# Weight splits by pairs of tiles, and attention steps by two chunks, in a fused attention and feed-forward kernel

## The chip, the cores and the metric

The kernel runs on one core of a Trainium2 chip. Its engines work in parallel, each through its own queue in order: TensorE (PE in the rows; PEld is its weight load), VectorE (DVE), ScalarE (ACT), GpSimd (POOL) and SyncE (SP), which here only issues transfers. The metric is the device time of one execution in microseconds.

## The reference

The program is a Performer attention layer followed by two feed-forward layers, on 4 batches of 8 heads with 576 tokens of width 64:

```python
def phi(x):                                   # 128 random features
    h = einsum('bhsd,md->bhsm', x, omega) - sum(x * x) / 2
    return exp(h - max(h)) / sqrt(m)
q_p, k_p = phi(q * scale), phi(k * scale)
kv = einsum('bhsm,bhsd->bhmd', k_p, v);  z = sum(k_p, axis=2)
x = (q_p @ kv) / (q_p @ z + 1e-6)             # then 2304 tokens x 512
x = ((x @ w_a) * (x @ w_b)) @ w_out           # 512 -> 1536 -> 512
h = maximum(x @ w_in, 0);  out = (h * h) @ w_out2    # 512 -> 2048 -> 512
```

The weights arrive as float64, all else as float32, and the result is float32.

## The kernel before

**Precision.** A product runs over high and low parts in a fast float32 format: three products (high-high, high-low, low-high, `TERMS`) make one. Every weight tile (128 rows, 512 values) is therefore split on the chip into such a pair by `split` (line 120): a load brings the raw 64-bit words as pairs of 32-bit integers, then three ScalarE and five VectorE instructions of 512 columns each make the high part `t[:, 0]` and the low part `t[:, 1]`, with three cut tiles `u`, `a` and `p` on the way (two buffers each). The raw tiles have two buffers too (`rawp`, line 79), each for one tile.

**Stages.** The first feed-forward layer works on 9 blocks of 256 tokens, in passes (`PASSES`, line 543): blocks 0 to 2 with the first six of twelve f tiles, the same blocks with the last six, blocks 3 to 6 one by one, and blocks 7 and 8 together. In a pass each f has three units: products with `w_a`, products with `w_b` (both line 561, tiles `ab`), and the products with `w_out` of two f earlier (line 585, tile `y`). The second layer (`b_units`, lines 716 and 704) follows over all tokens.

**Attention beside it.** Attention is cut into lanes: `k_steps` makes the features of k for a pair of heads (four chunks of 128 tokens) and the sums `ps_kv`; `q_steps` makes the features of q, chunk by chunk: `proj`, then `feat` (two transposes, a copy `qT`), `num` (numerators `ps_n` and `quotient`), and `turn` (transposes into `x_all`, the input of the first layer; one `turn` serves the chunks that lie in one block, a "group"). The 64 tokens left of a sequence are the tail steps `kt_steps` and `qt_steps`. Some features go in full float32 (`WIDE`, line 33: `phi_wide`, a 128x256 product, a minimum over its columns, one exponential per head), the others by high and low parts (`proj`, line 293).

**Order.** Before the first pass, `start_lanes` runs the lanes that block 0 needs, and at every 12th step (`SD`, line 828) `get_first` loads and splits a weight tile. In the passes, `SIDES` (line 751) names the lanes that are spread over the units of a pass by their counted steps, `W_AT` how many weights are loaded in each, and in the last pass `get_w2` (line 795) loads one tile of the second layer's weights per unit. A scheduling layer sets the final order of each engine's queue from this code and from the buffers of each pool; a tile's next use waits until its last use has ended.

Of the kernel before, what the change touches and what calls it, by code (L numbers as in the profile page):

```python
# [10 lines left out]
I32 = mybir.dt.int32  # L11
# [33 lines left out]
def kernel(  # L45
# [59 lines left out]
    def load_cols(w, f):  # L105
        t = rawp.tile([128, 512, 2], I32, tag="raw", name="raw")
        nc.sync.dma_start(
            out=t.rearrange("p (k f) w -> p k (f w)", k=KC),
            in_=w[:, f * 256:(f + 1) * 256].rearrange("(k p) f -> p k f", p=128),
        )  # L110
        return t

    def load_rows(w, f):
        t = rawp.tile([128, 512, 2], I32, tag="raw", name="raw")
        nc.sync.dma_start(
            out=t.rearrange("p f w -> p (f w)"), in_=w[f * 128:(f + 1) * 128, :]
        )
        return t

    def split(raw, pool, tag):  # L120


        up = raw[:, :, 1]
        t = pool.tile([128, 2, 512], F32R, tag=tag, name=tag)
        u = cutp.tile([128, 512], F32, tag="u", name="u")
        a = cutp.tile([128, 512], F32, tag="a", name="a")
        p = cutp.tile([128, 512], F32, tag="p", name="p")
        nc.scalar.activation(out=a, in_=f32(up), func=ACTF.Copy, scale=WORD_SCALE)  # L128
        nc.vector.tensor_scalar(
# [7 lines left out]
        nc.scalar.copy(out=t[:, 0, :], in_=p)  # L137
        nc.scalar.activation(
            out=i32(u), in_=raw.bitcast(U16)[:, :, 1],
            func=ACTF.Copy, scale=2.0 ** 7,  # L140
        )
# [72 lines left out]
    def tail_turn(nm, b, g):  # L214

        ps = at_bank([128, 128], "ps_tt")
        nc.tensor.transpose(ps, tails[nm, b][:, g].rearrange("t h d -> t (h d)"), ident)
        st = ap2.tile([128, 128], F32, tag=f"T{nm}", name="T", bufs=1)
        nc.scalar.copy(out=st, in_=ps)
        return st  # L220

    def phi_wide(s, dst):

        nm = ap2.tile([128, 2], F32, tag="nm", name="nm", bufs=4)
        ps = at_bank([128, 2, M], "ps_p")
# [11 lines left out]
    class Side:  # L237
# [44 lines left out]
        def proj(self, i, dst):  # L282
# [15 lines left out]
            nc.scalar.copy(out=c, in_=ps[:, :, 1, :])  # L298
# [622 lines left out]
```

## Time and profile before

| what | value |
|---|---|
| time, median of 3 runs (lowest to highest) | 1080.52 us (1079.51 to 1081.36) |
| profiled execution: own time, span | 1076.06 us, 1074.3 us |
| TensorE busy | 1047.3 us, 97% of the span |
| VectorE busy | 554.1 us, 1546 instructions |
| ScalarE busy | 487.4 us, 1179 instructions |
| mean granted clock of TensorE | 0.993 |

The span runs from the first to the last instruction; the execution's own time also has what lies around it. A busy TensorE is not TensorE at its peak, since the ends of pipelined products are modelled. A granted clock of 1.00 is 2.4 GHz; where a stretch has less, the lower level of 1.2 GHz was granted in part of it. In the rows by stage the engines stand in the order TensorE, its weight loads, VectorE, ScalarE, GpSimd. In the chain of waits each piece is what the next one waited for, up to the end. A group of instructions has its count, its busy time and the mean of one.

### The profile page before, as it was taken

How to read it: one execution, taken by the hardware profiler on the slowest of the kernel's cores; microseconds unless marked ns; L12 is line 12 of the kernel's file. 1: busy time of each engine (PE TensorE's matmuls, PEld its weight loads, DVE VectorE, ACT ScalarE, POOL GpSimd, SP SyncE). 2: the span in 40 equal slices, each digit the busy share in tenths (PEclk: the TensorE clock that was granted, in tenths of full speed). 3: DMA queues.
4: the chain of work that ended last, by engine and by line, in shares of the span. 5: the costliest groups of instructions: out<-in, count | busy, mean ns of one | idle time of the engine just before them, and what ended most of it. 6: DMA issues, size and time to landing. Idle time of an engine off the chain costs nothing.

```text
span 1074.3 us, 17147 instructions
## 1 busy us (share of the span) xinstructions
PE 1047.3 (97%) x6505; PEld 928.2 (86%) x6505; DVE 554.1 (52%) x1546; ACT 487.4 (45%) x1179; POOL 29.2 (3%) x54
## 2 busy tenths in 40 slices
PE   5998999999999999999999999999999999999998
PEld 4797989999999999999998888788788788778887
DVE  5887888766655433444458878522322322222222
ACT  6886768654455533433346656422322322322232
POOL 3100101000000000000000000000000000000000
PEclk9998999999999999999999999999999999999999
DMA  7855875862543333333438665300200200100010
GB/s 190 237 139 181 237 239 166 269 186 89 157 129 101 92 123 124 118 109 103 124 108 268 221 188 160 96 0 1 79 1 1 69 1 1 49 1 0 1 41 20
DMA packets 105555, 118.64 MB, mean 110 GB/s; under 512 B 55808, under 2 KB 84480, under 8 KB 105472
## 3 DMA queue, kind: packets, MB, share of 16 engines
q1 hardware_dynamic: 103936, 115.96, 35.5%
q0 software_dynamic: 1536, 1.58, 0.6%
q8 instruction: 52, 0.85, 0.3%
q14 instruction: 31, 0.25, 0.1%
HBM read 100.20 MB, written 17.30 MB: 109 GB/s over the span
## 4 chain that ended last, share of the span: by engine, by line
PE 90%; DMA 3%; ACT 3%; DVE 2%; issue 1%; SPq 0%; ACTq 0%
PE ab L561 22%; PE o L704 18%; PE ph L716 17%; PE y L585 13%; PE abw L561 6%; PE ps_p L293 3%; PE ps_n L426 3%; PE ps_kv L365 3%; PE ps_p L226 2%; PE ps_qt L418 2%; DMA out_dram<-o_s 1%; PE ps_t L271 1%; DMA raw<-in_moe_w_b_dram 1%; PE ps_x L436 1%; DMA raw<-in_moe_w_a_dram 1%
## 5 line engine op out<-in xcount | busy, mean ns | idle before, releaser
L561 PE MATMUL ab<-x_all,w 128*128 128x256 f32 x2016 | 298.0, 292 | 0.4 <-DVE x_all L499 0.3
L561 PEld LDWEIGHTS ab<-x_all,w 128*128 128x128 f32 x2016 | 263.8, 191 | 2.1 <-DVE x_all L499 0.5
L716 PE MATMUL ph<-yx,w 128*128 128x512 f32 (+1 forms) x840 | 185.5, 371 | 0.0
L585 PE MATMUL y<-gs,wo 128*128 128x256 f32 (+1 forms) x1152 | 181.4, 302 | 0.0
L704 PE MATMUL o<-w,ss 128*128 128x512 f32 x702 | 172.5, 392 | 2.8 <-ACT ss L725 2.8
L716 PEld LDWEIGHTS ph<-yx,w 128*128 128x128 f32 x840 | 148.1, 188 | 29.5
L724 DVE TENSOR_TENSOR r<-r 128x512 f32<-128x512 f32 (+1 forms) x80 | 51.1, 638 | 225.3 <-ACT r L723 225.3
L585 PEld LDWEIGHTS y<-gs,wo 128*128 128x128 f32 x1152 | 156.6, 190 | 7.2 <-DVE gs L645 0.3
L704 PEld LDWEIGHTS o<-w,ss 128*128 128x128 f32 x702 | 130.3, 188 | 33.4 <-ACT ss L725 4.2
L723 ACT ACTIVATE r<-ph 128x512 f32<-128x512 f32 (+1 forms) x80 | 44.3, 554 | 214.3 <-PE ph L716 214.3
L726 DVE TENSOR_TENSOR ss<-r,ss 128x512 fp32r<-128x512 f32 (+1 forms) x80 | 51.1, 639 | 48.0 <-ACT ss L725 41.9
L725 ACT CAST ss<-r 128x512 fp32r<-128x512 f32 (+1 forms) x80 | 46.2, 577 | 52.7 <-DVE r L724 52.7
L642 ACT ACTIVATE a_s<-ab 128x256 f32<-128x256 f32 x84 | 32.2, 384 | 81.7 <-PE ab L561 81.4
L561 PE MATMUL abw<-x_all,w 128*128 128x512 f32 x288 | 69.2, 395 | 0.0
L561 PEld LDWEIGHTS abw<-x_all,w 128*128 128x128 f32 x288 | 53.9, 188 | 13.0
L128 ACT ACTIVATE a<-raw 128x512 f32<-128x512 f32 x68 | 46.1, 678 | 26.9 <-DMA raw<-in_moe_w_out_dram 8.1
L644 ACT CAST gs<-a_s 128x256 fp32r<-128x256 f32 (+1 forms) x96 | 41.7, 435 | 30.7 <-DVE a_s L643 30.3
L643 DVE TENSOR_TENSOR a_s<-ab,a_s 128x256 f32<-128x256 f32 x84 | 35.2, 420 | 38.6 <-ACT a_s L642 38.1
L300 DVE CUSTOM_DVE_ANT_0 c<-ps_p,c 128x128 f32<-128x128 f32 x160 | 39.7, 287 | 23.5 <-ACT c L298 23.3
L645 DVE TENSOR_TENSOR gs<-a_s,gs 128x256 fp32r<-128x256 f32 (+1 forms) x96 | 43.6, 455 | 11.4 <-ACT gs L644 9.2
L142 DVE SCALAR_TENSOR_TENSOR u<-raw,u 128x512 uint32<-128x512 uint32 x68 | 46.6, 685 | 1.2
L133 DVE SCALAR_TENSOR_TENSOR p<-a,p 128x512 int32<-128x512 int32 x68 | 46.7, 686 | 0.9
(103 smaller groups left out, 1185.3 us busy)
## 6 DMA issues: line engine op xcount, KB each, us to landing
wo<-wo_d SPq DMA_DIRECT2D x84, 512.0 KB, 3.4
raw<-in_moe_w_out_dram SPq DMA_DIRECT2D x28, 512.0 KB, 3.9
raw<-in_moe_w_in_dram SPq DMA_DIRECT2D x16, 512.0 KB, 4.4
raw<-in_moe_w_a_dram SPq DMA_DIRECT2D x12, 512.0 KB, 4.4
raw<-in_moe_w_b_dram SPq DMA_DIRECT2D x12, 512.0 KB, 4.8
wo_d<-wo SPq DMA_DIRECT2D x12, 512.0 KB, 4.2
kn<-in_k_dram SPq DMA_DIRECT2D x16, 256.0 KB, 4.6
V<-in_v_dram SPq DMA_DIRECT2D x16, 256.0 KB, 3.4
```

What stands on the lines that cost most here:

```text
L128: nc.scalar.activation(out=a, in_=f32(up), func=ACTF.Copy, scale=WORD_SCALE)
L133: nc.vector.scalar_tensor_tensor(out=i32(p), in0=i32(a), scalar=-0x80000000, in1=i32(p), op0=ALU.bitwise_and, op1=ALU.bitwise_or,)
L142: nc.vector.scalar_tensor_tensor(out=u.bitcast(U32), in0=up.bitcast(U32), scalar=23, in1=u.bitcast(U32), op0=ALU.logical_shift_left, op1=A ...
L561: nc.tensor.matmul(ps, lhsT=wv[:, s_, kc, :], rhs=x[..., kc, m_, :], start=(kc == 0 and (s_, m_) == TERMS[0]), stop=(kc == KC - 1 and (s_, ...
L585: nc.tensor.matmul(y_part(pi, f, c), lhsT=wo[pi, f][:, s_, c * 128:(c + 1) * 128], rhs=g[:, m_, :],  start=(f == f0 and (wide or c % 2 == ...
L645: nc.vector.tensor_tensor(out=g[:, 1, :], in0=a_s, in1=f32(g[:, 0, :]), op=ALU.subtract)
L704: nc.tensor.matmul(op[t], lhsT=s_t[f][:, s_, t * 128:(t + 1) * 128], rhs=wo2[f][:, m_, :], start=(f == 0 and (s_, m_) == TERMS[0]), stop=( ...
L716: nc.tensor.matmul(ps, lhsT=wv[:, s_, kc, :], rhs=y[:, kc, m_, :], start=(kc == 0 and (s_, m_) == TERMS[0]), stop=(kc == KC - 1 and (s_, m ...
L723: nc.scalar.activation(out=r, in_=ps, func=ACTF.Relu, scale=1.0 / W_SCALE)
L724: nc.vector.tensor_tensor(out=r, in0=r, in1=r, op=ALU.mult)
L725: nc.scalar.copy(out=s_t[f][:, 0, :], in_=r)
L726: nc.vector.tensor_tensor(out=s_t[f][:, 1, :], in0=r, in1=f32(s_t[f][:, 0, :]), op=ALU.subtract)
```

## The change

A pair of tiles is loaded into one raw tile and split by the same eight instructions, 1024 columns wide (`get_pair`): `w_a[f]` with `w_b[f]`, and `w_in[f]` with `w_out2[f]` of the second layer. `w_out` of the first layer is still split tile by tile. `u` is no longer a tile of its own: it is written into the low words of the raw tile. The raw pool keeps two buffers, each now for two tiles; `a` and `p` have one buffer, for two tiles.

`phi_wide` takes up to two chunks: a product each into one PSUM tile, then one minimum over both. `q_steps` works by groups: `feat`, `num`, `quotient` and the copy `qT` take all chunks of a group (one or two) at once. Chunk 0 of q in batch 1 goes over to full float32. Weight loads ahead of the first pass come at every 8th step (a pair takes two turns, of which the second is empty), and `get_w2` loads a pair per f.

```diff
-    wpool = ctx.enter_context(tc.tile_pool(name="wpool", bufs=2 * FA))
+    wpool = ctx.enter_context(tc.tile_pool(name="wpool", bufs=FA))
     rawp = ctx.enter_context(tc.tile_pool(name="rawp", bufs=2))
-    cutp = ctx.enter_context(tc.tile_pool(name="cutp", bufs=2))
+    cutp = ctx.enter_context(tc.tile_pool(name="cutp", bufs=1))
...
-    def split(raw, pool, tag):
-        up = raw[:, :, 1]
-        t = pool.tile([128, 2, 512], F32R, tag=tag, name=tag)
-        u = cutp.tile([128, 512], F32, tag="u", name="u")
-        a = cutp.tile([128, 512], F32, tag="a", name="a")
-        p = cutp.tile([128, 512], F32, tag="p", name="p")
+    def split(raw, t):
+        n = raw.shape[1]
+        up = raw[:, :, :, 1]
+        u = raw[:, :, :, 0]
+        a = cutp.tile([128, 2, 512], F32, tag="a", name="a")[:, 0:n]
+        p = cutp.tile([128, 2, 512], F32, tag="p", name="p")[:, 0:n]
         nc.scalar.activation(out=a, in_=f32(up), func=ACTF.Copy, scale=WORD_SCALE)
+        nc.scalar.activation(
+            out=u, in_=raw.bitcast(U16)[:, :, :, 1], func=ACTF.Copy, scale=2.0 ** 7,
+        )
...
-        nc.scalar.copy(out=t[:, 0, :], in_=p)
-        nc.scalar.activation(
-            out=i32(u), in_=raw.bitcast(U16)[:, :, 1],
-            func=ACTF.Copy, scale=2.0 ** 7,
-        )
+        nc.scalar.copy(out=t[:, :, 0, :], in_=p)
...
+    def get_pair(pool, tag, *parts):
+        t = pool.tile([128, 2, 2, 512], F32R, tag=tag, name=tag)
+        split(load(*parts), t)
+        return t[:, 0], t[:, 1]
...
-    def phi_wide(s, dst):
+    def phi_wide(rows, dst):
+        n = 2 * len(rows)
-        ps = at_bank([128, 2, M], "ps_p")
-        nc.tensor.matmul(
-            ps.rearrange("p h m -> p (h m)"), lhsT=s,
-            rhs=OMZ.rearrange("p h m -> p (h m)"), start=True, stop=True,
-        )
+        ps = at_bank([128, n, M], "ps_p")
+        for x, s in enumerate(rows):
+            nc.tensor.matmul(
+                ps[:, 2 * x:2 * x + 2].rearrange("p h m -> p (h m)"), lhsT=s,
+                rhs=OMZ.rearrange("p h m -> p (h m)"), start=True, stop=True,
+            )
         nc.vector.tensor_reduce(out=nm, in_=ps, axis=AXX, op=ALU.min)
...
-            self.wide = (nm, b) in WIDE
+            self.wide = (nm, b) in WIDE or (nm, b) == ("q", 1) and 0 in chunks
...
-        def feat(u):
-            ps = at_bank([128, 2, 128], "ps_qt")
-            for h in range(2):
-                nc.tensor.transpose(ps[:, h, :], qp[u][:, h, :], ident)
-            qT = ap2.tile([128, 2, 128], F32, tag="qT", name="qT", bufs=2)
+        def feat(g, t):
+            ps = at_bank([128, 2 * len(g), 128], "ps_qt")
+            for x in range(2 * len(g)):
+                nc.tensor.transpose(ps[:, x, :], t["qp"][:, x, :], ident)
+            t["qT"] = ap2.tile([128, 2 * len(g), 128], F32, tag="qT", name="qT", bufs=1)
...
-        for u in units:
-            qp[u] = ap2.tile([128, 2, M], F32, tag="qp", name="qp", bufs=2)
-            qs.proj(u, qp[u])
-            yield
-            for _ in range(min(2, len(todo))):
-                todo.pop(0)()
+        for g in groups:
+            t = {"qp": ap2.tile([128, 2 * len(g), M], F32, tag="qp", name="qp", bufs=2)}
+            for _ in qs.proj(g, t["qp"]):
                 yield
...
-            o = cutp.tile([128, DM], F32, tag="a", name="o_s")
+            o = op_pool[0].tile([128, DM], F32, tag="o", name="o_s")
...
     def get_w(f):
-        wa[f] = split(load_cols(w_a, f), wpool, "w")
-        wb[f] = split(load_cols(w_b, f), wpool, "w")
+        wa[f], wb[f] = get_pair(wpool, "w", (w_a, f, False), (w_b, f, False))
...
-    S0, SD = 1, 12
+    S0, SD = 1, 8
```

Two places of the order follow. The first is the head of ScalarE's queue; `OMS`, `OMZ` and `OM` are the scaled omega, `S` a transposed block of k or q, `a`, `u` and `w` the split. Before:

```order
L128 ACT_TABLE_LOAD
L128 ACTIVATE a<-raw 128x512
L191 ACTIVATE OMS<-ps_om 128x128
L194 ACTIVATE OMZ<-ps_om 64x128 x2
L195 CAST OM<-OMS 128x128
L138 ACTIVATE u<-raw 128x512
L277 COPY S<-ps_t_156 128x512
L137 CAST w<-p 128x512
L219 COPY T<-ps_tt 128x128
L128 ACTIVATE a<-raw 128x512
```

And of the change:

```order
L198 ACTIVATE OMS<-ps_om 128x128
L201 ACTIVATE OMZ<-ps_om 64x128 x2
L202 CAST OM<-OMS 128x128
L131 ACTIVATE a<-raw 128x1024
L132 ACTIVATE raw<-raw 128x1024
L287 COPY S<-ps_t_156 128x512
L226 COPY T<-ps_tt 128x128
L287 COPY S<-ps_t_216 128x256
L132 ACTIVATE raw<-raw 128x512
L143 CAST w<-p 128x2x512
```

The split moved behind the scaling of omega, and its first two instructions, now of a pair, stand directly ahead of the first copy `S`.

The second place is SyncE's queue in the first pass, where the weights of its last f are loaded; `wo_d` is the store of a split `w_out` tile, `qn`, `kn` and `V` the inputs of attention. Before:

```order
L251 DMA kn<-in_k_dram 128x8x64
L115 DMA raw<-in_moe_w_out_dram 128x1024
L107 DMA raw<-in_moe_w_a_dram 128x4x256
L351 DMA V<-in_v_dram 128x8x64
L254 DMA qn<-in_q_dram 128x64
L107 DMA raw<-in_moe_w_b_dram 128x4x256
L254 DMA qn<-in_q_dram 128x64
L787 DMA wo_d_84<-wo 128x1024
L115 DMA raw<-in_moe_w_out_dram 128x1024 x2
```

And of the change:

```order
L112 DMA raw<-in_moe_w_out_dram 128x1024
L261 DMA kn<-in_k_dram 128x8x64
L116 DMA raw<-in_moe_w_a_dram 128x4x256
L116 DMA raw<-in_moe_w_b_dram 128x4x256
L365 DMA V<-in_v_dram 128x8x64
L797 DMA wo_d_84<-wo 128x1024
L112 DMA raw<-in_moe_w_out_dram 128x1024
L264 DMA qn<-in_q_dram 128x64 x4
L112 DMA raw<-in_moe_w_out_dram 128x1024
```

The load of `w_b` moved up to stand at once behind `w_a`, ahead of the loads of `V` and `qn`.

## Rows read from the trace of the kernel before

**Rows 1.** Busy us by stage: engines (instructions), granted clock, DMA share, GB/s

```profile
0.00:47.00 47.00, 34.73 (x205) 27.70 (x205) 33.31 (x91) 36.19 (x105) 12.46 (x26) 1.00 0.79 204
47.00:100.00 53.00, 48.95 (x338) 44.97 (x337) 42.80 (x123) 38.19 (x103) 1.17 (x2) 0.90 0.55 160
100.00:156.00 56.00, 53.27 (x413) 50.34 (x411) 50.59 (x153) 41.47 (x111) 8.50 (x14) 1.00 0.78 237
156.00:200.00 44.00, 43.77 (x354) 43.33 (x355) 34.23 (x108) 33.42 (x88) 4.78 (x8) 0.97 0.64 200
200.00:560.00 360.00, 358.85 (x2900) 346.83 (x2899) 185.33 (x723) 159.00 (x458) 2.32 (x4) 1.00 0.41 127
...
664.00:1074.30 410.30, 403.74 (x1836) 330.49 (x1835) 121.82 (x197) 115.72 (x209) 0.00 (x0) 1.00 0.09 27
```

**Rows 2.** The same view of two short stretches

```profile
86.00:96.00 10.00, 7.41 (x28) 6.22 (x28) 7.05 (x20) 5.31 (x15) 0.00 (x0) 0.56 0.27 99
...
156.00:160.00 4.00, 4.00 (x23) 4.00 (x24) 3.17 (x10) 2.83 (x6) 0.00 (x0) 0.64 0.79 301
```

**Rows 3.** Chain of waits near 80 us: start, us, piece

```profile
79.75 0.35 SPq L254
80.19 4.90 DMA raw<-in_moe_w_b_dram
```

**Rows 4.** Timeline of TensorE from 86 to 94 us, with the idle time before

```profile
86.65 0.58 PE L418 MATMUL ps_qt<-ident,qp 128*128 128x128 f32 x2 [1.82 <-ACT qp L232]
...
93.68 1.84 PE L561 MATMUL ab<-x_all,w 128*128 128x256 f32 x6
```

**Rows 5.** Chain of waits from 146 to 160 us

```profile
146.45 0.60 DVE p L133
...
155.93 4.18 PE ab L561 x22
```

**Rows 6.** Groups by form: busy us, mean ns of one, idle before

```profile
L133 DVE SCALAR_TENSOR_TENSOR p<-a,p 128x512 int32<-128x512 int32 x68 | 46.7, 686 | 0.9
L128 ACT ACTIVATE a<-raw 128x512 f32<-128x512 f32 x68 | 46.1, 678 | 26.9 <-DMA raw<-in_moe_w_out_dram 8.1 <-DMA raw<-in_moe_w_a_dram 7.3 <-DMA raw<-in_moe_w_in_dram 4.4
L642 ACT ACTIVATE a_s<-ab 128x256 f32<-128x256 f32 x84 | 32.2, 384 | 81.7 <-PE ab L561 81.4
L230 DVE TENSOR_REDUCE nm<-ps_p 128x2 f32<-128x256 f32 x64 | 26.3, 418 | 6.9 <-PE ps_p L226 6.5
L402 DVE TENSOR_TENSOR xh<-ps_n,den 128x128 f32<-128x128 f32 x64 | 18.3, 286 | 1.2
L398 DVE TENSOR_SCALAR den<-ps_n 128x2 f32<-128x2 f32 x64 | 10.1, 158 | 36.2 <-PE ps_n L426 35.9
L642 ACT ACTIVATE a_s<-abw 128x512 f32<-128x512 f32 x12 | 7.2, 596 | 16.5 <-PE abw L561 16.5
L265 DVE TENSOR_TENSOR S<-ps_t,S 64x256 fp32r<-64x256 f32 x16 | 6.8, 426 | 0.4
L265 DVE TENSOR_TENSOR S<-ps_t,S 64x512 fp32r<-64x512 f32 x8 | 5.5, 694 | 0.2
```

**Rows 7.** Chain pieces: ten full-float32 products, two products by parts

```profile
35.99 2.30 PE ps_p L226 x10
...
160.11 0.24 PE ps_p L293 x2
```

**Rows 8.** Start: timeline, then issues of 0 to 20 us (median us to landing)

```profile
4.10 0.51 SPq L107 DMA_DIRECT2D raw<-in_moe_w_b_dram  x1
8.99 0.66 ACT L128 ACTIVATE a<-raw 128x512 f32<-128x512 f32 x1 [6.97 <-DMA raw<-in_moe_w_a_dram]
11.17 0.58 ACT L277 COPY S<-ps_t 128x512 f32<-128x512 f32 x1
...
raw<-in_moe_w_b_dram SPq DMA_DIRECT2D x1, 512.0 KB, 6.9
```

**Rows 9.** Chain of waits at the end of the last pass

```profile
666.31 4.88 DMA raw<-in_moe_w_in_dram
```

More of the change, by code (lines that the diff above doesn't have):

```diff
@@ new lines, in proj @@
+            for n, o in enumerate(oo):
+                nm = ap2.tile([128, 2], F32, tag="nm", name="nm", bufs=4)
+                ps = at_bank([128, 2, 2, M], "ps_p")
+                for x in range(2):
+                    nc.tensor.matmul(
+                        ps[:, x].rearrange("p a m -> p (a m)"), lhsT=self.s[:, x, o:o + 128],
+                        rhs=OM.rearrange("p a m -> p (a m)"), start=True, stop=True,
+                    )
+                c = ap2.tile([128, 2, M], F32, tag="c", name="c", bufs=2)
+                nc.scalar.copy(out=c, in_=ps[:, :, 1, :])
+                for x in range(2):
+                    nc.vector.tensor_tensor_reduce(
+                        out=c[:, x, :], in0=ps[:, x, 0, :], in1=c[:, x, :], scale=1.0,
+                        scalar=3.0e38, op0=ALU.add, op1=ALU.min, accum_out=nm[:, x:x + 1],
+                    )
+                for x in range(2):
+                    nc.scalar.activation(
+                        out=dst[:, 2 * n + x, :], in_=c[:, x, :], func=ACTF.Exp, scale=-1.0,
+                        bias=nm[:, x:x + 1],
+                    )
+                yield
@@ L358, in k_steps @@
         kp = ap1.tile([128, 8, M], F32, tag="kp", name="kp")
-        for i in range(4):
-            ks.proj(i, kp[:, 2 * i:2 * i + 2, :])
-            yield
+        for i in range(0, 4, 2):
+            yield from ks.proj((i, i + 1), kp[:, 2 * i:2 * i + 4, :])
         ps = at_bank([128, 2, D + 1], "ps_kv")
@@ L391, in layout, with quotient @@
         return units, col, groups
[L393 to L397 removed]
+    def quotient(v_, r0, r1, xh):
+        n = v_.shape[1]
+        den = ap2.tile([128, n, 1], F32, tag="den", name="den", bufs=3)[r0:r1]
         nc.vector.tensor_scalar(
@@ L785, in get_wo @@
             wo_made.add(f)
-            wo[pi, f] = split(load_rows(w_out, f), wop, "wo")
+            wo[pi, f] = wop.tile([128, 2, 512], F32R, tag="wo", name="wo")
+            split(load((w_out, f, True)), wo[pi, f].unsqueeze(1))
             nc.sync.dma_start(out=wo_d[f], in_=f32(wo[pi, f]))
-    w2_list = [(x, f) for f in range(FB) for x in (0, 1)]
-    W2_L, W2_R = 3, 2 * (FB - FA) - 3
+    W2_L, W2_R = 1, FB - FA - 1
     w2 = {"n": 0}
     def get_w2():
-        n = w2["n"]
-        if n >= len(w2_list):
+        f = w2["n"]
+        if f >= FB:
             return
         w2["n"] += 1
-        x, f = w2_list[n]
-        if n < W2_L:
+        if f < W2_L:
             po = (w2["l"], "w2")
-        elif n < W2_L + 2 * FA:
+        elif f < W2_L + FA:
             po = (wpool, "w")
@@ L815, in get_first @@
         for f in range(W_FIRST):
-            wa[f] = split(load_cols(w_a, f), wpool, "w")
+            get_w(f)
             yield
-            wb[f] = split(load_cols(w_b, f), wpool, "w")
             yield
```

133 lines of the change are left out of this document (55 added, 78 removed).

## The prediction

> **What bounds the kernel now.** I read the busy time by stage first, then the small stretches in which a stage falls short, then the chain of waits and the instructions there, and last the groups of equal instructions for the prices.
>
> The stages [rows 1] show TensorE busy for 358.85 of 360 us between 200 and 560 us, and the page has it at 97% of the whole span. There and in the last 410 us (6.6 us idle) nothing that VectorE or ScalarE saves can be worth more than those idle microseconds. Before 200 us it is otherwise. In the first 47 us, where the first attention features are made and no product of block 0 runs yet, TensorE is busy for 34.73 us and ScalarE for 36.19 us; ScalarE has work from about 9 us on, so it is busy for 36 of 38 us. Between 47 and 100 us TensorE is idle for 4.05 us, and its granted clock is 0.90 in the mean: with the lower of its two levels (1.2 against 2.4 GHz) granted for part of the time, 0.10 x 53 = 5.3 us of work are lost on top. Between 100 and 200 us it is idle for 2.73 + 0.23 us, and 0.03 x 44 = 1.3 us go to the clock.
>
> So what can be won in the middle is 4.05 + 5.3 = 9.3 us in the first product pass and 2.73 + 0.23 + 1.3 = 4.3 us behind it, 13.6 us together. Both losses sit in one place each [rows 2]: from 86 to 96 us the granted clock is 0.56 and TensorE is busy for 7.41 of 10 us, and from 156 to 160 us the clock is 0.64 behind a wait.
>
> The first place is read from the chain and from the instructions [rows 3, 4]. SyncE's queue holds the load of w_b for the last f of the pass behind a load of q that itself waits for a transpose; it is issued at 80.19 us, lands 4.9 us later, and ScalarE's first instruction of that split stands in its queue ahead of the exponentials that TensorE needs, so TensorE waits 1.82 us at 86.65. The next products of that pass start at 93.68 us, when the split is through, and six of them take 1.84 us, at the lower clock. The second place is VectorE alone [rows 5]: from 146.45 us on the chain is on its split instructions, the cuts of the next k block and the quotients of the tail rows, and the 22 products of line 561 start behind them at 155.93 us.
>
> **The change part by part.** *Splits by pairs.* w_a with w_b, and w_in with w_out of the second layer, make 28 pairs; 12 tiles of the first w_out stay single. A split has five VectorE and three ScalarE instructions. The trace has no tile 1024 wide. From below a pair's instruction could cost what one does now (686 ns, row L133 of rows 6), from above two of them (1372 ns). Nearest is the slope between two widths: 256 more columns cost 694 - 426 = 268 ns on VectorE and 596 - 384 = 212 ns on ScalarE [rows 6]. So a pair costs 686 + 536 = 1222 ns on VectorE (0.15 us saved) and 678 + 424 = 1102 ns on ScalarE (0.25 us saved). I take 5 x 0.15 = 0.75 us for the pair on VectorE and 3 x 0.25 = 0.75 us on ScalarE, 21 us on each over the run. That u is now written back into every second word is a form that the trace does not have; line 128 reads such words already in its 678 ns, and I add nothing.
>
> *Minima, transposes, numerators and quotients by two chunks.* Of the q groups 24 hold two chunks (six in each of four head pairs), 16 hold one. A pair saves one 158 ns instruction, one reciprocal that I take to cost the same, and 2 x 286 - (286 + 134) = 152 ns of the product with it: 0.47 us on VectorE. One minimum of 128x256 costs 418 ns [rows 6], so two as one save 0.15 us; 24 pairs of k and q have them. That is 24 x 0.62 = 15 us of VectorE, and with the copies of the transposes about 40 us of its 554 and 23 of ScalarE's 487. None of it lies on the path from 200 us on.
>
> *q of batch 1, chunk 0, goes over to full float32.* Four head pairs with one chunk each lose two products by parts, 0.24 us, and get one full product, which the trace has as two records of 230 ns (ten in 2.30 us) [rows 7]: 4 x 0.22 = +0.9 us on TensorE. VectorE and ScalarE lose some cuts for it, which I leave at nothing.
>
> *The first 47 us.* ScalarE's order now has the first split behind the scaling of omega, but the split of the pair needs both loads. The load of w_b is issued 0.9 us behind that of w_a, at 4.10 us, and took 6.9 us [rows 8], so it lands at 11.0 us instead of 8.99. Behind it stand the two wide ScalarE instructions of the pair, 2.2 us, and then the copy S that the first feature product waits for: at about 13.2 us, where it stands at 11.17 now. That is +2.0 us. Against it, this stage saves 2 x 0.75 + 4 x 0.15 = 2.1 us on ScalarE and 2 x 0.75 + 4 x 0.47 + 12 x 0.15 = 5.2 us on VectorE. ScalarE is the fuller one, so the term is 0, between +2.0 (nothing is won back) and -3.2 (VectorE's saving counts).
>
> *The first product pass.* Loads now stand in SyncE's queue as pairs, w_b at once behind w_a, and two raw tiles hold four weights, not two: w_b of the last f no longer waits for the split of another tile or for a load of q. VectorE's work there falls by 4 x 0.75 + 4 x 0.47 + 8 x 0.15 = 6.1 us of 42.80, so the splits that the products wait for are through earlier. Of the 9.3 us I take 7, with 0 and 9.3 as ends; what is late next is the attention steps themselves, whose TensorE work is bigger at a time now.
>
> *The second place.* The chain of rows 5 loses 0.75 us for one pair, and in the new order the first instruction of a further pair stands ahead of the x_all of that block: -1 us, between 0 and -4.3.
>
> *New waits.* The cut tiles have one buffer, not two, so ScalarE's first instruction of a split waits for VectorE's last of the split before, and behind it in ScalarE's queue stand the exponentials and the copies that TensorE's next transposes and numerators wait for. Every split instruction is also 0.54 us longer for what stands behind it. Some 18 splits (11 pairs, 7 single tiles, counted in the order) lie before 160 us; at the far end each costs TensorE those 0.54 us, 9.7 us, at the near end nothing since products of line 561 stand in between. I take +1.5 us.
>
> *The last pass.* At 666 us ScalarE waits for a load of w_in for 4.88 us of the chain [rows 9], and TensorE loses about a microsecond before the second layer starts. With a pair loaded ahead I take -0.5 us, between 0 and -1. The output tiles get a pool of their own with the same two buffers, so the waits for output transfers at the block ends stay: 0.
>
> *The sum:* 0 - 7 - 1 + 1.5 - 0.5 + 0.9 = -6.1 us. Made against the profiled execution (span 1074.3, own time 1076.06 us) that is about 1070.0; the median of the runs, 1080.52, lies 4.5 us above that execution, and against it the forecast is 1074.4 us, with its own range of 1069 to 1078.
>
> **The rivals.** *Slower: wide instructions and the single cut buffer block the queues in front of TensorE.* Price: 18 splits at 0.54 us are 9.7 us, the late start 2.0, the wide q 0.9; against it half of the 9.3 us, and 1.5 us of the second place and the last pass: +6.4, so 1087 us. It decides from the point where a split costs TensorE more than (7 + 1 + 0.5 - 0.9) / 18 = 0.42 us. For it speaks that TensorE's wait of 1.82 us [rows 4] came from just such a queue; against it that VectorE's and ScalarE's load falls by 7% and 5%. The Trainium skill's page "Perfetto Trace Analysis", section "Optimizing Scalar/DVE Operations", states the rule behind this rival: where these engines are not saturated but hold up others, breaking instructions up may let work complete sooner. By that rule the change goes the wrong way wherever the engines have slack, which by rows 1 is everywhere but before 156 us.
>
> *No change.* The stall at 86 us is set by the transposes that hold SyncE's queue and by the time that loads take to land, and comes back at another f: then 0 + 0 - 1 + 1.5 - 0.5 + 0.9 = +0.9, about 1081 us. For it speaks that the late load was itself behind a load of q; against it the deeper buffer. That the change does not pair what it says is ruled out by the rows of its order.
>
> *Faster than forecast.* With VectorE 40 us lighter no stall is left between 47 and 200 us (-13.6), and the first stage keeps VectorE's net gain (-3.2): with +0.9 that is -15.9, so 1064.6 us. Against it speaks that ScalarE, not VectorE, is the fuller engine in the first stage.
>
> **How the numbers follow.** Forecast 0.52, slower 0.18, no change 0.14, faster still 0.16. A difference under 0.2% (2.2 us) can't be told from none here. The forecast's own range is faster by that measure, so faster has 0.68, same 0.14, slower 0.18. The range from 1064 to 1082.5 holds the forecast, the case of no change, about half of the faster case and the near part of the slower one: 0.52 + 0.14 + 0.09 + 0.05 = 0.80.
>
> **What would show it.** Right: the granted clock between 47 and 100 us near 1.0 and TensorE idle there for under 2 us; a pair's VectorE instruction at 1.2 us and ScalarE's at 1.1; VectorE's busy time near 514 us; the first feature product near 13.2 us. Wrong: TensorE idle longer than now between 47 and 160 us with waits for exponentials or for copies of transposes; a stretch of half clock at another place; ScalarE waiting for VectorE's last split instruction; or a first product of line 561 later than 49 us.

## The result and the profile after

| | before | after |
|---|---|---|
| median of 4 runs each, same chip | 1080.01 us (1077.91 to 1081.36) | 1070.76 us (1068.43 to 1072.73) |
| profiled execution: own time, span | 1076.06, 1074.3 us | 1070.55, 1068.8 us |
| TensorE / VectorE / ScalarE busy | 1047.3 / 554.1 / 487.4 us | 1042.4 / 529.5 / 475.7 us |

The ratio is 0.9915, 95% interval 0.9889 to 0.9941: faster by 9.25 us in the medians, by 5.5 us in the two profiled spans (the profiled execution before lies about 4 us below the median of its runs). The forecast of 1074.4 us is 3.6 us high.

The stages of the changed kernel, then the two short stretches, with the columns of [rows 1, 2]:

```profile
0.00:47.00 47.00, 33.81 (x186) 27.07 (x186) 30.11 (x58) 33.15 (x87) 12.71 (x26) 1.00 0.76 192
47.00:100.00 53.00, 52.33 (x398) 48.95 (x398) 45.08 (x95) 42.07 (x101) 3.51 (x6) 1.00 0.62 182
100.00:156.00 56.00, 51.09 (x392) 48.06 (x391) 45.92 (x99) 37.99 (x87) 5.85 (x10) 1.00 0.81 245
156.00:200.00 44.00, 43.95 (x366) 43.24 (x365) 28.07 (x89) 29.12 (x76) 4.66 (x8) 1.00 0.53 159
200.00:560.00 360.00, 356.60 (x2883) 344.67 (x2883) 180.61 (x659) 160.48 (x456) 2.32 (x4) 1.00 0.42 130
664.00:1068.80 404.80, 400.66 (x1830) 329.58 (x1828) 123.58 (x190) 117.07 (x205) 0.00 (x0) 1.00 0.09 29
...
86.00:96.00 10.00, 10.00 (x80) 9.50 (x79) 9.02 (x21) 8.07 (x19) 2.34 (x4) 1.00 0.29 87
156.00:160.00 4.00, 4.00 (x37) 4.00 (x35) 3.60 (x19) 3.55 (x13) 0.00 (x0) 1.00 0.76 250
```

Read them against [rows 1, 2] by what TensorE loses: idle time, plus the clock's shortfall times the length of the stretch. From 47 to 100 us it lost 4.05 + 5.3 and now loses 0.67; the half clock of 86 to 96 us is gone. From 100 to 156 us the idle time rose from 2.73 to 4.91 us, from 156 to 200 us idle time and clock together fell from 1.5 to 0.05, from 200 to 560 us idle time rose from 1.15 to 3.40 us, and from 664 us on it fell from 6.6 to 4.1. In the first 47 us it is 0.9 us more.

Two waits of TensorE make the new idle time behind 100 us. ScalarE's timeline, then TensorE's, with the idle time before and what ended it:

```profile
108.43 1.15 ACT L131 ACTIVATE a<-raw 128x1024 f32<-128x1024 f32 x1 [1.61 <-DMA raw<-in_moe_w_b_dram]
125.17 1.14 ACT L132 ACTIVATE raw<-raw 128x1024 int32<-128x1024 uint16 x1 [1.11 <-DMA raw<-in_moe_w_b_dram]
```

```profile
112.30 0.70 PE L236 MATMUL ps_p<-OMZ,S 128*128 128x256 f32 x2 [1.72 <-ACT S L287]
127.63 0.44 PE L378 MATMUL ps_kv<-V,kp 128*128 128x65 f32 x2 [0.94 <-ACT kp L242]
```

ScalarE stood idle until a pair's `w_b` had landed and then ran two wide instructions; the copy S and the features `kp` that TensorE waited for came behind them. In the chain of waits three loads of `w_b` stand where the chain of before had none that long (4.77 us at 126.19); of the three, only the second has a wait of TensorE right behind it:

```profile
104.93 8.14 DMA raw<-in_moe_w_b_dram
117.39 7.70 DMA raw<-in_moe_w_b_dram
137.33 5.45 DMA raw<-in_moe_w_b_dram
```

The prices of the new forms, with the columns of [rows 6]:

```profile
L139 DVE SCALAR_TENSOR_TENSOR p<-a,p 128x1024 int32<-128x1024 int32 x28 | 34.2, 1222 | 0.5
L131 ACT ACTIVATE a<-raw 128x1024 f32<-128x1024 f32 x28 | 32.2, 1152 | 12.4 <-DMA raw<-in_moe_w_b_dram 7.6 <-DMA raw<-in_moe_w_out_dram 3.4 <-DVE w L152 0.9
L240 DVE TENSOR_REDUCE nm<-ps_p 128x4 f32<-128x512 f32 x24 | 16.5, 689 | 7.5 <-PE ps_p L236 7.2
L414 DVE TENSOR_TENSOR xh<-ps_n,den 128x256 f32<-128x256 f32 x24 | 10.1, 423 | 0.6
L413 DVE RECIPROCAL den<-den 128x4 f32<-128x4 f32 x24 | 4.2, 176 | 0.6
```

1222 ns is the forecast to the nanosecond; ScalarE's 1152 ns is 50 more than forecast. The wait for `w` (L152), the single cut buffer's, is 0.9 us in all here, and 1.5 us in the group of the 12 single tiles.

The start, in the timeline (start, length, instruction, idle before); it answers to [rows 8]:

```profile
10.83 1.12 ACT L131 ACTIVATE a<-raw 128x1024 f32<-128x1024 f32 x1 [5.98 <-DMA raw<-in_moe_w_b_dram]
12.35 0.66 PE L281 MATMUL ps_t<-ident,qn 128*128 128x128 f32 x2 [5.64 <-DMA qn<-in_q_dram]
13.01 0.59 ACT L287 COPY S<-ps_t 128x512 f32<-128x512 f32 x1
13.65 3.78 PE L236 MATMUL ps_p<-OMZ,S 128*128 128x256 f32 x8 [0.64 <-ACT S L287]
...
47.76 1.09 PE L570 MATMUL ab<-x_all,w 128*128 128x256 f32 x7
```

The copy S starts at 13.01 us (forecast: 13.2) and ends at 13.60; the first feature product follows at 13.65, where 13.2 was named and 11.80 stood before. The first product of block 0 comes at 47.76 us, 0.96 us later than before (46.80).

### The profile page after: what moved, and what is told of

Same layout as the page of the kernel before. It is cut to its first block, busy times and chain, and to the rows that moved or that the text cites. A ratio compares the mean times of both kernels' runs of the same rounds, so it can differ in the third digit from the quotient of the medians.

```text
span 1068.8 us, 16733 instructions
## 1 busy us (share of the span) xinstructions
PE 1042.4 (98%) x6505; PEld 926.1 (87%) x6505; DVE 529.5 (50%) x1274; ACT 475.7 (45%) x1079; POOL 29.1 (3%) x54
## 4 chain that ended last, share of the span: by engine, by line
PE 87%; DMA 5%; ACT 4%; DVE 3%; issue 1%; SPq 1%; ACTq 0%; DVEq 0%
PE ab L570 19%; PE o L714 19%; PE ph L726 18%; PE y L594 12%; PE abw L570 6%; PE ps_kv L378 2%; PE ps_p L306 2%; PE ps_n L436 2%; PE ps_p L236 2%; DMA raw<-in_moe_w_b_dram 2%; DMA raw<-in_moe_w_out_dram 2%; PE ps_qt L429 2%; PE ps_t L281 1%; ACT raw L132 1%; PE ps_x L447 1%
## 5 line engine op out<-in xcount | busy, mean ns | idle before, releaser
L570 PE MATMUL ab<-x_all,w 128*128 128x256 f32 x2016 | 286.9, 288 | 0.6 <-ACT x_all L453 0.5
L570 PEld LDWEIGHTS ab<-x_all,w 128*128 128x128 f32 x2016 | 258.1, 189 | 1.7 <-ACT x_all L453 0.7
L594 PE MATMUL y<-gs,wo 128*128 128x256 f32 (+1 forms) x1152 | 184.9, 303 | 0.0
L726 PE MATMUL ph<-yx,w 128*128 128x512 f32 (+1 forms) x780 | 172.3, 371 | 0.0
L726 PEld LDWEIGHTS ph<-yx,w 128*128 128x128 f32 x780 | 137.5, 188 | 27.4
L131 ACT ACTIVATE a<-raw 128x1024 f32<-128x1024 f32 (+1 forms) x40 | 40.4, 1010 | 18.3 <-DMA raw<-in_moe_w_out_dram 7.8
L144 DVE SCALAR_TENSOR_TENSOR raw<-raw 128x1024 uint32<-128x1024 uint32 (+1 forms) x40 | 42.5, 1063 | 11.6 <-ACT raw L132 11.4
L132 ACT ACTIVATE raw<-raw 128x1024 int32<-128x1024 uint16 (+1 forms) x40 | 40.7, 1018 | 11.3 <-DMA raw<-in_moe_w_out_dram 9.1
```

The costliest lines, as they stand in the source:

```text
L132: nc.scalar.activation(out=u, in_=raw.bitcast(U16)[:, :, :, 1], func=ACTF.Copy, scale=2.0 ** 7,)
L144: nc.vector.scalar_tensor_tensor(out=u.bitcast(U32), in0=up.bitcast(U32), scalar=23, in1=u.bitcast(U32), op0=ALU.logical_shift_left, op1=A ...
L570: nc.tensor.matmul(ps, lhsT=wv[:, s_, kc, :], rhs=x[..., kc, m_, :], start=(kc == 0 and (s_, m_) == TERMS[0]), stop=(kc == KC - 1 and (s_, ...
L594: nc.tensor.matmul(y_part(pi, f, c), lhsT=wo[pi, f][:, s_, c * 128:(c + 1) * 128], rhs=g[:, m_, :],  start=(f == f0 and (wide or c % 2 == ...
L726: nc.tensor.matmul(ps, lhsT=wv[:, s_, kc, :], rhs=y[:, kc, m_, :], start=(kc == 0 and (s_, m_) == TERMS[0]), stop=(kc == KC - 1 and (s_, m ...
```

## The experiments

"First product" is the first of block 0, "lost" TensorE's idle time plus the clock's shortfall, in one profiled execution each, worked out from the clock at the two decimals of the rows and so good to 0.4 us. The ratios are to the kernel before on the same chip.

| kernel | ratio (95% interval) | first product | lost 0-47 | 47-100 | 100-200 | 200-300 |
|---|---|---|---|---|---|---|
| before | 1 | 46.80 | 12.3 | 9.3 | 4.7 | 0.3 |
| changed | 0.9915 (0.9889-0.9941) | 47.76 | 13.2 | 0.7 | 5.0 | 2.3 |
| e1 pairs, attention as before | 1.0085 (1.0066-1.0104) | 53.77 | 17.7 | 1.1 | 13.8 | 4.9 |
| e10 = e1, weight step 8 | 1.0071 (1.0047-1.0095) | 56.43 | 21.7 | 1.5 | 9.0 | 1.5 |
| e12 = e1, split by tiles | 0.9998 (0.9981-1.0014) | 51.38 | 15.1 | 1.5 | 2.4 | 5.9 |
| e2 chunks, splits as before | 0.9925 (0.9902-0.9947) | 45.55 | 13.5 | 2.6 | 2.9 | 0.2 |
| e9 = e2, instructions apart | 0.9934 (0.9910-0.9958) | 49.70 | 15.1 | 3.4 | 1.5 | 0.8 |
| e11 = e2, four raw tiles | 1.0001 (0.9985-1.0017) | 46.39 | 14.6 | 1.0 | 3.2 | 4.5 |
| e5 = changed, split by tiles | 0.9905 (0.9889-0.9921) | 49.60 | 17.3 | 2.8 | 0.9 | 4.8 |
| e4 = changed, one raw pair | 1.0340 (1.0317-1.0363) | 50.26 | 14.9 | 16.2 | 13.5 | 16.1 |
| e6 = changed, first split later | 0.9886 (0.9867-0.9906) | 46.06 | 13.3 | 1.6 | 3.1 | 1.9 |
| e7 = changed, loads a unit ahead | 0.9926 (0.9911-0.9941) | 50.23 | 16.8 | 0.4 | 5.0 | 2.0 |
| e8 = changed, q by parts | 0.9920 (0.9900-0.9941) | 47.40 | 13.7 | 0.7 | 5.1 | 1.9 |
| e3 = before, output pool | 0.9999 (0.9982-1.0016) | 47.51 | 11.8 | 7.2 | 6.1 | 0.3 |

**e1: the pairs alone.** The attention functions, the weight step and `WIDE` of before in the changed kernel:

```diff
-            yield from ks.proj((i, i + 1), kp[:, 2 * i:2 * i + 4, :])
+            ks.proj(i, kp[:, 2 * i:2 * i + 2, :])
...
-        for g in groups:
+        for u in units:
...
-    S0, SD = 1, 8
+    S0, SD = 1, 12
```

> The changed kernel with attention as before: one chunk at a time, q of batch 1 chunk 0 by parts, a weight step every 12 units as before. Left of the change: loads and splits by pairs, one cut buffer, output tiles in a pool of their own. Theory (the loads as pairs and four weights in raw tiles make the first product pass): 47 to 100 us at a clock of 1.0 with under 2 us idle, second layer about 2 us shorter, so 0.992 to 0.995 of before. Rival (the attention steps by two chunks make it, by VectorE's smaller load): half clock stays between 86 and 96 us, and only the 2 to 2.5 us of the second layer are won: 0.997 to 0.998.

Measured: 1087.2 us, slower than before by 9 us. What the theory said of the first pass holds, and its time does not. From e1, then from the changed kernel, two stretches in the columns of the stages:

```profile
24.00:40.00 16.00, 14.93 (x76) 12.25 (x74) 11.66 (x32) 12.34 (x35) 2.39 (x4) 0.79 0.67 169
70.00:100.00 30.00, 29.72 (x233) 28.29 (x232) 25.73 (x65) 22.44 (x58) 1.17 (x2) 1.00 0.47 139
```

```profile
24.00:40.00 16.00, 14.30 (x91) 11.53 (x90) 12.83 (x26) 14.69 (x42) 3.74 (x6) 1.00 0.72 201
70.00:100.00 30.00, 30.00 (x234) 28.55 (x233) 26.24 (x63) 22.47 (x56) 2.34 (x4) 1.00 0.56 166
```

From 70 to 100 us both are full. But e1 has a new stretch of half clock between 24 and 40 us: TensorE is busy for as long as in the changed kernel and gets 76 products through, not 91. More is lost between 140 and 172 us:

```profile
140.00:172.00 32.00, 26.35 (x162) 22.47 (x161) 24.85 (x74) 20.42 (x52) 2.37 (x4) 0.79 0.58 177
```

That the first pass is cleared is no effect of the later start: from its first product to the first one of the next pass (53.77 to 99.62 us) TensorE loses 0.3 us in e1.

**e2: the chunks alone**, the reverse: attention, `WIDE` and weight step of the changed kernel in the kernel before.

```diff
-            ks.proj(i, kp[:, 2 * i:2 * i + 2, :])
+            yield from ks.proj((i, i + 1), kp[:, 2 * i:2 * i + 4, :])
...
-    S0, SD = 1, 12
+    S0, SD = 1, 8
```

> The kernel before with attention by two chunks alone (with q of batch 1 chunk 0 in full float32, and a weight step every 8 units of the shorter start list); loads and splits by single tiles, two cut buffers, output tiles in the cut pool. Theory (loads): the wait for the late w_b near 86 us and the half clock stay: within 2 us of before, 0.998 to 1.002. Rival (VectorE's smaller load): 5 to 7 us faster in 47 to 100 us, 0.993 to 0.996, with the clock at 1.0 there.

Measured: 1069.05 us, and 70 to 100 us are full here too:

```profile
70.00:100.00 30.00, 29.92 (x233) 28.49 (x233) 27.40 (x72) 23.57 (x62) 2.33 (x4) 1.00 0.59 181
```

The rival wins: nearly all of the change's gain is here, without a pair. Whether VectorE's smaller load makes it is e9's question. The step of 8 came in together with the groups and was not run alone in the kernel before; on the shorter start list it leaves the loads about where they were (the second `w_a` and `w_b` are issued at 20.52 and 23.99 us, before at 19.47 and 23.16). The third part, q of batch 1, is e8's question.

**e9: the same order, the merged instructions taken apart.**

```diff
-        nc.vector.tensor_reduce(out=nm, in_=ps, axis=AXX, op=ALU.min)
+        for x in range(0, n, 2):
+            nc.vector.tensor_reduce(out=nm[:, x:x + 2], in_=ps[:, x:x + 2], ...)
-            quotient(pn, 0, 128, t["xh"])
+            for x in range(0, 2 * len(g), 2):
+                quotient(pn[:, x:x + 2], 0, 128, t["xh"][:, x:x + 2])
```

(the copy `qT` likewise)

> As the kernel with attention by two chunks alone (e2), in the same order of steps, but with the merged instructions taken apart again: two minima, two copies of transposes and two quotients (three instructions each) a group. Theory 1 (VectorE's and ScalarE's saved work, about 15 us on VectorE, makes the gain of e2): back to 0.997 to 1.0 of before. Theory 2 (the new order makes it: products and transposes of two chunks in a row, fewer steps of attention between two steps of the weights): stays at 0.9915 to 0.995.

Measured: 1071.8 us. The page's first lines, e2 and then e9:

```profile
PE 1041.0 (98%) x6505; PEld 925.1 (87%) x6505; DVE 539.9 (51%) x1414; ACT 484.9 (45%) x1163; POOL 29.0 (3%) x54
```

```profile
PE 1042.2 (98%) x6505; PEld 925.3 (87%) x6505; DVE 549.8 (51%) x1526; ACT 484.9 (45%) x1171; POOL 29.0 (3%) x54
```

VectorE has 9.9 of the 14.2 us of work back that e2 had saved, and the ratio moves from 0.9925 to 0.9934, within both intervals. So the gain comes with the order of the steps by groups, not with the work saved.

**e12: e1 with the pair split tile by tile.** Loads stay back to back in the order and u stays in place; raw and cut tiles are single ones in the same memory.

```diff
-    rawp = ctx.enter_context(tc.tile_pool(name="rawp", bufs=2))
-    cutp = ctx.enter_context(tc.tile_pool(name="cutp", bufs=1))
+    rawp = ctx.enter_context(tc.tile_pool(name="rawp", bufs=4))
+    cutp = ctx.enter_context(tc.tile_pool(name="cutp", bufs=2))
...
-        split(load(*parts), t)
+        raws = [load(x) for x in parts]
+        for x, raw in enumerate(raws):
+            split(raw, t[:, x:x + 1])
```

> As e1 (pairs, attention by one chunk, 1.0085 of before), with the edit of e5: a pair's two loads still go back to back, into four single raw tiles, but the split goes tile by tile with two cut buffers. Theory (the wide instructions on ScalarE stand in front of exponentials that TensorE waits for, as at 25 us in e10, and the idle stretch brings half clock): the loss goes, 0.993 to 1.0 of before, first product of block 0 before 50 us, no half clock between 24 and 40 us. Rival (loads back to back, or u in place, cost it): 1.005 to 1.010, the first product later than 52 us.

Measured: 1079.69 us, so the edit is worth 0.0087 x 1079 = 9.4 us to e1, and the intervals are apart. It takes out several things at once: the width of the instructions, the wait of a split for both loads of its pair, and the single cut buffer. The stretch of half clock is gone:

```profile
24.00:40.00 16.00, 12.98 (x88) 10.38 (x86) 13.17 (x39) 14.05 (x44) 3.30 (x6) 1.00 0.81 231
```

The first product came at 51.38 us, later than the theory's 50. And the first pass is clean here too (1.5 us lost), yet the kernel is no faster than before: 2.8 us more are lost in the first 47 us and 5.6 more from 200 to 300. There ScalarE stands at a load, with the work on S behind it that TensorE needs:

```profile
216.62 0.65 ACT L132 ACTIVATE raw<-raw 128x512 int32<-128x512 uint16 x1 [2.92 <-DMA raw<-in_moe_w_out_dram]
219.10 0.62 PE L302 MATMUL ps_p<-OM,S 128*128 128x256 f32 x3 [3.66 <-DVE S L273]
```

This loss is not the width's, which e12 does not have. Every version that writes `u` into the raw tile, which is then busy until the split's last instruction, loses about 1.5 us or more from 200 to 300 us; the four with `u` in a tile of its own (before, e2, e9, e3) lose 0.2 to 0.8. The former also have two buffers for `a_s`, the scaled products of the first layer, in place of three, an edit of the change that the section on it does not name; no run takes the two apart.

**e10: e1 with the weight step at 8**, to see whether the step made e1's loss.

```diff
-    S0, SD = 1, 12
+    S0, SD = 1, 8
```

> As the kernel with pairs alone (e1, 1.0085 of before), but with a weight step every 8 units of the start list, as the changed kernel has it, not every 12. Theory (e1 lost its time to the pairs meeting the attention steps of one chunk, behind the start as well): within 4 us of e1, 1.005 to 1.012, first product of block 0 later than 50 us. Rival (the step of 12 put the pairs badly into the start list): 0.995 to 1.0, the first product before 48 us.

Measured: 1087.3 us, the first product at 56.43 us: it did not. This trace has the loss in its plainest form. TensorE's timeline, then ScalarE's, then the short stretches:

```profile
25.02 0.60 PE L233 MATMUL ps_p<-OMZ,S 128*128 128x256 f32 x2
27.21 0.59 PE L425 MATMUL ps_qt<-ident,qp 128*128 128x128 f32 x2 [1.59 <-ACT qp L239]
```

```profile
25.27 1.12 ACT L131 ACTIVATE a<-raw 128x1024 f32<-128x1024 f32 x1 [0.81 <-DVE nm L237]
26.28 0.62 ACT L239 ACTIVATE kp<-ps_p,nm 128x128 f32<-128x128 f32 x2
26.78 0.64 ACT L239 ACTIVATE qp<-ps_p,nm 128x128 f32<-128x128 f32 x2
```

```profile
24.00:26.00 2.00, 1.62 (x9) 1.06 (x7) 1.52 (x5) 1.19 (x3) 0.00 (x0) 1.00 1.25 259
26.00:28.00 2.00, 0.59 (x2) 0.28 (x2) 1.73 (x4) 2.00 (x8) 0.00 (x0) 1.00 1.22 325
28.00:30.00 2.00, 1.75 (x9) 1.75 (x9) 1.17 (x3) 2.00 (x6) 0.00 (x0) 0.56 0.71 289
30.00:32.00 2.00, 2.00 (x12) 2.00 (x11) 0.24 (x2) 1.76 (x4) 0.00 (x0) 0.50 0.00 0
...
36.00:38.00 2.00, 1.94 (x6) 0.95 (x5) 0.89 (x4) 1.84 (x5) 1.84 (x4) 0.50 0.94 222
```

The pair's first ScalarE instruction, 1.12 us, stands in front of the exponentials; TensorE waits 1.59 us for one, is busy for 0.59 of 2 us, and then has half clock until about 38 us (0.68 in the mean from 24 to 40), which is 0.32 x 16 = 5.1 us. The width is not all of it: ScalarE was idle for 0.81 us before, and the pair's second load landed at 25.20 us, its first at 23.61. And in e1 the half clock of 24 to 40 us comes another way: TensorE's two waits ahead of it are over at 28.23 us, and the first wide instruction of the stretch starts at 28.11.

```profile
26.79 0.66 PE L433 MATMUL ps_n<-kvr,qT 128*128 128x65 f32 x4 [0.45 <-ACT qT L427]
28.11 1.24 ACT L131 ACTIVATE a<-raw 128x1024 f32<-128x1024 f32 x1
28.23 0.33 PE L443 MATMUL ps_x<-ident,xh 128*128 128x128 f32 x1 [0.55 <-DVE xh L409]
```

So neither trace shows that the width alone makes the loss; e12 shows what its edit as a whole is worth.

**e5: the changed kernel with the pair split tile by tile** (the edit of e12).

> The changed kernel, in which a pair is still loaded at once, into four single raw tiles, but split tile by tile with two cut buffers: the same memory, the same loads, u still in place, and only the width of the split's instructions undone. Theory 1 (width costs: what stands behind a wide instruction on ScalarE and VectorE waits longer than it saves): 2 to 5 us faster than the changed kernel, 0.986 to 0.990 of before. Theory 2 (width pays, by the 0.15 to 0.2 us that each wide instruction saves): 3 to 6 us slower than the changed kernel, 0.994 to 0.997. Between them, 0.990 to 0.993: width is worth nothing here.

Measured: 1069.58 us, 0.9905 against 0.9915. With attention by groups the same edit costs and saves nothing that can be told in the time. By stage it does something: without the width 0.9 us are lost from 100 to 200 us, not 5.0 (with single chunks 2.4, not 13.8), but 4.1 us more in the first 47.

**e4: one raw pair, e11: four raw tiles on e2.** How deep the loads go; the first edit is e4's, the second e11's:

```diff
-    rawp = ctx.enter_context(tc.tile_pool(name="rawp", bufs=2))
+    rawp = ctx.enter_context(tc.tile_pool(name="rawp", bufs=1))
```

```diff
-    rawp = ctx.enter_context(tc.tile_pool(name="rawp", bufs=2))
+    rawp = ctx.enter_context(tc.tile_pool(name="rawp", bufs=4))
-        u = cutp.tile([128, 512], F32, tag="u", name="u")
+        u = raw[:, :, 0]
...
-            a_s = gp.tile([128, w_], F32, tag="t", name="a_s")
+            a_s = gp.tile([128, w_], F32, tag="t", name="a_s", bufs=2)
...
-    W2_L, W2_R = 3, 2 * (FB - FA) - 3
+    W2_L, W2_R = 2, 2 * (FB - FA) - 2
```

> The changed kernel with one raw pair tile, not two: two weights in flight as in the kernel before, same work on every engine. Theory (depth of the loads): a load waits for the split of the pair before, landing shows up as waits of ScalarE for raw, half clock comes back in the first product pass: 5 to 9 us slower than the changed kernel, 0.996 to 1.0 of before. Rival (work saved on VectorE and ScalarE): at most 2 us slower than the changed kernel, 0.991 to 0.9935 of before.

> As e2 (attention by two chunks, splits tile by tile, each load at its split), with four raw tiles in place of two; u goes back into the raw words to make room, and one w2 tile fewer lies on the left side. Theory (what the pairs bring is the depth of the loads alone): 1 to 3 us faster than e2, 0.989 to 0.9915 of before, with the wait for w_a behind 49 us (2.5 idle us in 47 to 70) gone. Rival (the depth is worth nothing once attention goes by two chunks): 0.992 to 0.9945.

Measured: 1115.12 us for e4, far over both numbers: one pair less makes waits in every stage up to 300 us. The theory has the sign of that, and no number of it fits. For more depth than two single tiles, e11 is inconclusive: it is 8 us slower than e2, but its edit moved a tile of the second layer's weights and took a buffer from `a_s` to make room, and it lost 4.3 us more from 200 to 300 us, and about 6 more from 660 to 840. The latter stretch, e2 and then e11:

```profile
660.00:840.00 180.00, 179.18 (x778) 145.50 (x777) 60.19 (x93) 55.54 (x95) 0.00 (x0) 1.00 0.12 36
```

```profile
660.00:840.00 180.00, 174.59 (x750) 141.41 (x749) 65.52 (x105) 57.67 (x98) 0.00 (x0) 0.99 0.13 41
```

**e6: the first split eight units behind its load.**

```diff
-            get_w(f)
-            yield
+            load_w(f)
+            yield
+            split_w(f)
             yield
```

> The changed kernel, where in the start list the split of a first weight pair is placed one step of the list (eight units) behind its load, not at once behind it. It tests the late start: theory, the copy S no longer stands behind the pair's first ScalarE instructions, the first feature product comes at 11 to 12 us in place of 13.65, and the first stage ends 1 to 3 us earlier: 0.9885 to 0.991 of before. Rival (ScalarE's and VectorE's work sets the end of that stage): the first product of block 0 stays at 48 us, within 1 us of the changed kernel.

Measured: 1067.47 us. The first feature product comes at 12.63 us and the first product of block 0 at 46.06, 1.7 us earlier, near what the theory has (11 to 12 us for the first). It has the lowest ratio of all and beats the kernel before by 11.7 us; against the changed kernel (0.9886 to 0.9915) the intervals overlap.

**e7: loads a unit ahead of their splits.**

```diff
+        split_late()
         if kind == "a":
...
-                get_w(w_next)
+                get_w_late(w_next)
```

`get_w_late` (and `get_wo`) issue the load and put the split on a list; `split_late`, at the next unit's start, issues it.

> The changed kernel, where behind the start list every load of a first-layer weight or w_out is placed one unit ahead of its split, and the store of a w_out split comes with the split. Theory (the pairs give back what they win in waits of ScalarE's queue for raw, 100 to 145 and 200 to 230 us): TensorE's 4.9 idle us in 100 to 156 and 2.3 in 200 to 300 fall to 2 together, 0.985 to 0.988 of before. Rival (these waits lie beside other work, the idle time has other causes): within 2 us of the changed kernel, 0.990 to 0.9935.

Measured: 1071.72 us; the rival holds. From 100 to 156 us:

```profile
100.00:130.00 30.00, 29.88 (x233) 28.69 (x232) 24.18 (x51) 21.87 (x56) 3.50 (x6) 1.00 0.89 274
130.00:156.00 26.00, 22.86 (x172) 21.34 (x171) 22.83 (x55) 16.85 (x34) 2.33 (x4) 0.97 0.85 255
```

The waits for w_b did stand behind the idle time up to 130 us, which falls from 2.75 to 0.12 us; behind it 3.14 us and some clock are lost, where the changed kernel lost 2.17. The idle time of this stage moves without any edit to these loads, too: e6 and e8 have 2.81 and 3.32 us from 100 to 156 us, the changed kernel 4.91.

**e8: q of batch 1, chunk 0 by parts again.**

```diff
-            self.wide = (nm, b) in WIDE or (nm, b) == ("q", 1) and 0 in chunks
+            self.wide = (nm, b) in WIDE
```

> The changed kernel with q of batch 1, chunk 0 by parts as before. Theory (full float32 there costs TensorE 0.9 us and buys nothing): 0 to 1 us faster than the changed kernel, 0.990 to 0.992 of before. Rival (the cuts that it saves on VectorE and ScalarE stand on the path in 100 to 156 us): 2 to 4 us slower than the changed kernel, 0.9935 to 0.996, with TensorE idle for 7 us or more in 100 to 156 us.

Measured: 1070.49 us, 0.9920 against 0.9915: neither the 0.9 us nor a gain on VectorE can be told.

**e3: the output pool alone**, in the kernel before.

```diff
-            o = cutp.tile([128, DM], F32, tag="a", name="o_s")
+            o = op_pool[0].tile([128, DM], F32, tag="o", name="o_s")
```

> The kernel before, with the two output tiles of the second layer in a pool of their own and nothing else. Theory (the place of the output tiles makes the shorter waits at the block ends): ScalarE's waits of o_s for output transfers fall from 9.7 to about 4.3 us and the time by about 2 us, 0.998 of before. Rival (the pairs do it, by loads and splits that are through earlier in the last layer): waits stay near 9.7 us, time within 0.5 us, 0.9995 to 1.0005.

Measured: 1077.44 us, 0.9999. Waits of ScalarE for output transfers from 838 to 1066 us, in total, times, longest: before, e3 and e2 (which keeps the output tiles in the cut pool):

```profile
ACT o_s L735 <- DMA out_dram<-o_s: 8.3, 3, 3.4
```

```profile
ACT o_s L736 <- DMA out_dram<-o_s: 5.0, 2, 3.0
```

```profile
ACT o_s L737 <- DMA out_dram<-o_s: 3.9, 4, 1.5
```

The waits do not go with the pool: e3, which has it, keeps 5.0 us of them, and e2, which does not, has 3.9. The 1.7 us that the changed kernel's profile shows at the block ends are not the pool's.

## Why the prediction was right, and where it was not

**The time was right, the step that carried it was not.** The prediction has the pairs win the first product pass, since loads go back to back into deeper raw tiles. The stretch was cleared to 0.7 us, more than the 7 of 9.3 us forecast. But the step that fails is the credit, "so the splits that the products wait for are through earlier. Of the 9.3 us I take 7", as a gain of the pairs: pairs alone (e1, e12) clear the pass and win nothing in all, and chunks alone (e2) clear it and win 8 us. The prediction has no term for the order of the attention steps, and that is what the gain comes with. That the sum, -6.1 us, lies near the 5.5 us of the two profiles, which it was made for, is in part luck. The stall of [rows 3, 4] was an accident of one order of steps: of the twelve experiments only e3, which keeps that order in the stages before, and e4 with its single raw pair lose more than 4 us there. A gain read off one stall is the whole kernel's only if no new stall comes elsewhere, and with pairs alone one came.

**First stage: 0, between +2.0 and -3.2.** The first feature product moved by +1.85 us and the first product of block 0 by +0.96. The mechanism given (both loads, the two wide instructions, then S) is there, but it is only part of it: in the new order two transposes of q, which wait for a load of q until 12.35 us, stand in TensorE's queue ahead of that product. e6, where S is copied at 6.69 us, still has it at 12.63, and e2, without a pair, at 13.17. In both, block 0 starts before 46.80 us all the same, so a late first feature product does not set the end of the stage.

**Second place: -1.** At its place right (156 to 160 us at full clock), by its stage wrong: TensorE's idle time from 100 to 156 us rose by 2.2 us, with the waits of 1.72 and 0.94 us behind wide instructions, which this term did not have and the next one put at 1.5 for the whole run.

**New waits: +1.5, and the slower rival.** In the changed kernel, width, joint wait and single cut buffer together make no difference that can be told (e5); 1.5 us lie within the intervals. The rise of 2.25 us from 200 to 560 us stands against "None of it lies on the path from 200 us on": it goes with `u` in the raw tile or the two buffers of `a_s`, which no term had. The slower rival is not ruled out as a mechanism: with attention by single chunks e12's edit is worth 9.4 us. That its price was 9.7 us is luck, for it counted 18 equal delays, while in e1 two stretches of half clock alone (24 to 40 and 140 to 172 us, 0.79 in each) make 0.21 x 48 = 10.1 us. Why the groups go with fewer stalls is not measured. One reading is that with a group's transposes and products in a row there is other work while ScalarE is at a wide instruction; against it, e7, with groups and wide splits, also has a granted clock of 0.79 from 24 to 40 us. The Trainium skill's rule that the prediction weighed ("Perfetto Trace Analysis", section "Optimizing Scalar/DVE Operations": unsaturated engines that hold up others may be better off with instructions broken up) is borne out by e12's time and not by e5's.

**Last pass -0.5, block ends 0.** From 664 us on 2.4 us less are idle; 0.7 of it lies before 840 us, the size of the term; but pairs alone lose more there, not less (from 664 to 840 us before 1.0 us idle, e1 2.2, e12 1.4, the changed kernel 0.3). The rest goes neither with the pool (e3) nor with the pairs (e2 has it without them); what makes it stays open.

**VectorE busy near 514 us.** It is 529.5. The busy times of its groups add up to 610.3 us before and 570.1 after, 40.2 us less, as worked out; the engine's busy time fell by 24.6, since instructions of neighbouring groups overlap: 0.15 us by group for each of the 272 instructions saved, but 0.09 us of the engine. The Trainium skill's page "Perfetto Trace Analysis", section "Optimizing Scalar/DVE Operations", says that a profiled latency is about twice the overhead that the engine is busy for, since half of it overlaps with the next instruction; the trace agrees (0.15 against 0.09), and the term left it out. ScalarE's busy time fell by 11.7 us, not 23. e9 says that VectorE's part mattered little.

**What stays open:** why half clock follows one idle stretch and not another (e12 is idle for 1.3 us between 24 and 28 us and keeps the full clock, e1 for 0.8 and has half clock from 29 us on); which part of the groups' order keeps TensorE fed; and how far the stage figures of one profiled execution would repeat.

## What to carry to other kernels

A stall read in one profile tells what one order of the queues happens to hit; before crediting an edit with it, ask whether any other reordering would clear it too, and what the edit puts in front of the bottleneck's other inputs. Widening instructions on engines that have slack won nothing that can be told here, and with it went a loss of 9 us where the attention steps were short: group the waiting engine's work first, and test the width by itself. Take instructions saved by the engine's busy time, not by the sum of durations.

## What the runs showed of the hardware

- Half clock can outlast the idle stretch that it follows: in e10 TensorE was idle for 1.59 us up to 27.21 us, and from 28 to 38 us its granted clock was 0.50 to 0.56 while it was busy for 9.1 of the 10 us.
- How long a load of 512 KB takes to land differs with its place. In the kernel before, the four loads of w_b issued from 100 to 145 us took 4.6 to 5.3 us; in the changed kernel the five took 5.3 to 8.1. Standing at once behind w_a does not decide it: the three issued within 0.5 us of it took 8.1, 7.7 and 5.3 us, and one issued 4.7 us behind it 7.3.
- On ScalarE, `a` and `u`, read from every second word of the raw tile, took 1152 and 1156 ns for 1024 columns, the cast from packed words to packed words 1050. The operations differ too, and no run takes the two apart.
